# Decayed keys through DRAM in 2 KB rows and back in 512 B runs, and the state update's products in four 32-column tiles, in a new order

## The chip, the cores and the metric

One core of one Trainium2 chip. The metric is device microseconds of one execution, and lower is better. A profile's span is about 1.8 us shorter than the time of the same execution, so spans are compared with spans and times with times. The *granted clock* is TensorE's clock in a trace as a share of full speed. The *slack* of a chunk is the other work that TensorE has between the write of its keys and their use.

## The reference, cut to what matters

```python
# q, k, v, alpha: (4, 8, 768, 48); w_in: 384 x 2048; w_out: 2048 x 384
for t in range(S):
    state = alpha[:, :, t, :, None] * state + np.einsum('bhd,bhe->bhde', k[:, :, t], v[:, :, t])
    y[:, :, t] = np.einsum('bhd,bhde->bhe', q[:, :, t], state)
# x = y as (3072 tokens, 384)
h = x @ w_in
g = h * np.clip(h + 3.0, 0.0, 6.0) / 6.0
return g @ w_out
```

The kernel works in 24 chunks of 128 tokens, six to a batch. For each chunk the recurrence needs a product of the decayed keys and the values, summed over tokens: the *update*, called `u` below. The keys come out of the decay with the head dimension on the partitions, and the update needs tokens there. So the keys must be turned. The two large products over `w_in` and `w_out` fill most of TensorE's time, and the recurrence is woven between them.

## The kernel before: the parts that matter

Chunks 0 to 4 turn their keys on TensorE (`k_by_token`, `keep_k`); chunk 5, like the last chunk of every batch, needs no update. Chunks from `FAR` on turn 32x32 blocks on VectorE (`turn_k`) and let the DMA carry the blocks to their places: out to DRAM (`write_k`), and back (`read_k`).

```python
    FAR = 6
    # V = 4 blocks of BLK = 32; C = 128; NP = 4 pairs of heads
    def write_k(j):
        far_t[j] = far.tile([BLK, V, NP, V, BLK], FP, tag="far", name="far")
        src = k_in_blocks(j).rearrange("r (v p c) -> r (v p) c", v=V, p=NP)
        to = far_t[j].rearrange("s v p o c -> o s (v p) c")
        for o in range(V):
            nc.sync.dma_start(out=to[o], in_=src[BLK * o : BLK * (o + 1)])

    def read_k(j):
        kb_t[j] = wk.tile([C, NP, C], FP, tag="kb", name="kb")
        nc.sync.dma_start(out=kb_t[j].rearrange("s p r -> s (p r)"),
                          in_=far_t.pop(j).rearrange("s v p o c -> v s (p o c)"))

    def update(j):
        ...
        for p in range(NP):
            for a in range(2):
                nc.tensor.matmul(u[64 * a : 64 * a + D, p, D * a : D * a + D],
                                 kb_t[j][:, p, 64 * a : 64 * a + D],
                                 vs[:, 2 * p + a, (64 - D) * a : (64 - D) * a + D],
                                 start=True, stop=True)
```

So 256 KB go out in four DMAs of 128 B runs, and come back in one DMA of 2 KB rows. The order of everything, on all engines and queues, is one hand-made list of short names (`lk.2` loads chunk 2's keys, `u.8` is chunk 8's update, `z` is a run of dummy matmuls that keep TensorE busy).

Of the kernel before, what the change touches and what calls it, by code (L numbers as in the profile page):

```python
# [8 lines left out]
FP = mybir.dt.float32  # L9
# [8 lines left out]
def kernel(  # L18
# [32 lines left out]
    nc = tc.nc  # L51
    B, H, S, D = q.shape
    NTOK, DM = out.shape
    C = 128
    NC = S // C
    NCH = B * NC
    NP = H // 2
# [3 lines left out]
    G = 2  # L61
# [310 lines left out]
    FAR = 6  # L372
# [9 lines left out]
    def write_k(j):  # L382
        far_t[j] = far.tile([BLK, V, NP, V, BLK], FP, tag="far", name="far")
        src = k_in_blocks(j).rearrange("r (v p c) -> r (v p) c", v=V, p=NP)
        to = far_t[j].rearrange("s v p o c -> o s (v p) c")
        for o in range(V):
            nc.sync.dma_start(out=to[o], in_=src[BLK * o : BLK * (o + 1)])

    def read_k(j):
        kb_t[j] = wk.tile([C, NP, C], FP, tag="kb", name="kb")  # L390
        nc.sync.dma_start(out=kb_t[j].rearrange("s p r -> s (p r)"),
                          in_=far_t.pop(j).rearrange("s v p o c -> v s (p o c)"))
# [8 lines left out]
    def update(j):  # L401
        if last(j):
            return
        u = bank("u", j).rearrange("r p n -> r (p n)")[:, 0 : NP * 2 * D].rearrange(
            "r (p n) -> r p n", p=NP)
        ps_t["u", j] = u
        vs = v_t[j]
        for p in range(NP):
            for a in range(2):
                nc.tensor.matmul(u[64 * a : 64 * a + D, p, D * a : D * a + D],  # L410
                                 kb_t[j][:, p, 64 * a : 64 * a + D],
                                 vs[:, 2 * p + a, (64 - D) * a : (64 - D) * a + D],
                                 start=True, stop=True)
# [323 lines left out]
    with tc.manual_schedule():  # L737
        run("""la.0 z.3.5 lq.0 lk.0 lk.1 ta.0 la.1 ca.0 tq.0 r.0 lv.0.0 tk.0 lq.2 p.0 tk.1 z.0.2
            la.2 k.0 ta.1 q.0 z.0.1 lq.1 ca.1 sc.0 r.1 la.3 tq.2 z.0.5 m.0 lv.3.1 k.1 w.1 ta.2
            p.1 tq.1 ca.2 kb.0 r.2 ck.0 ta.3 u.0 ca.3 z.0.2 q.1 sm.0 sc.1 lv.1.2 p.2 la.4 kb.1  # L740
            m.1 st.1 z.0.4 ck.1 lk.2 d2.1 r.3 yi.0 w.3 d1.1 z.0.4 d3.1 cy.0 dx.1 ta.4 yi.1 q.2
            p.3 tk.2 yx.1 lk.3 k.2 d4.1 cy.1 u.1 lv.2.0 sc.2 sm.1 w.0 st.2 fa.1.0 d2.3 m.2 d1.3
            kb.2 d3.3 fb.1 ck.2 u.2 lq.3 fr.0.1 yi.2 d4.3 sm.2 w.4 fg.0.1 tk.3 st.3 f.0.3.1 k.3
            d2.0 d1.0 d3.0 ca.4 tq.3 dx.0 lq.4 r.4 yx.2 z.0.5 la.5 q.3 cy.2 d4.0 fr.0.3 sc.3
            lk.5 fg.0.3 d2.4 kb.3 m.3 w.2 d1.4 fa.0.2 dx.4 d3.4 yi.3 p.4 tk.5 yx.3 d4.4 w.5 fb.0
            cy.3 tq.4 fr.0.0 f.1.4.3 q.4 d2.2 fg.0.0 d1.2 d3.2 lq.5 dx.2 f.1.3.0 w.6 fr.1.4 d4.2
            d2.5 fg.1.4 ta.5 fa.4.1 fr.1.3 d3.5 ca.5 d1.5 w.7 f.1.2.2 r.5 fa.2.3 d2.6 fg.1.3
            d4.5 k.5 d1.6 fb.4 d3.6 w.8 f.0.5.0 fr.0.4 fr.1.2 fg.0.4 d4.6 d2.7 fg.1.2 d1.7
            f.1.5.1 d3.7 fr.0.5 w.9 fb.2 p.5 fr.1.5 d2.8 fg.1.5 d4.7 tq.5 d1.8 f.0.6.2 fg.0.5
            lk.4 q.5 fr.0.2 d3.8 w.10 ck.3 f.1.7.1 fr.0.6 fg.0.2 d2.9 d4.8 fg.0.6 d1.9 lv.4.2  # L750
            d3.9 f.0.7.0 fr.1.7 w.11 fg.1.7 d4.9 tk.4 d2.10 u.3 k.4 fr.0.7 sc.5 d3.10 d1.10
            f.1.0.3 w.12 fg.0.7 d4.10 sm.3 b.0.0.2 m.5 d2.11 st.4 fr.1.0 lv.5.0 d3.11 d1.11 w.13
            sc.4 fg.1.0 b.1.0.1 d4.11 d2.12 m.4 d1.12 d3.12 w.14 kb.4 yi.5 ck.4 d4.12 u.4
            f.1.1.0 sm.4 d2.13 st.5 d1.13 w.15 d3.13 yx.5 fr.1.1 yi.4 cy.5 fg.1.1 d2.14 f.1.6.3
            d4.13 d1.14 lk.6 d3.14 yx.4 fr.1.6 la.6 b.1.1 cy.4 fg.1.6 d4.14 d2.15 d1.15 lq.6
            d3.15 b.0.1 xc.2.1 la.7 tk.6 d4.15 b.1.2 ca.6 x.0 b.0.2 y.1 y.5 y.6 y.2 b.1.3 y.3
            y.7 y.4 y.8 y.9 b.0.3 bo.1 y.10 so.1 y.11 y.15 y.13 P.1.1.0 bo.0 s.1.0.0 so.0
            s.1.1.1 s.1.2.2 s.1.3.3 M.2.15.3 s.1.4 P.1.0.1 x.1 y.16 P.1.3.2 x.2 K.1.0 y.0 x.3
            P.1.2 K.1.2 y.17 y.12 M.2.16 y.19 K.1.1 y.18 P.1.4 y.20 y.21 xc.2.3 y.23 xc.2.4
            G.1.0 xc.2.5 O.1.0 G.1.1 M.2.0.0 xc.2.6 O.1.1 s.1.5 P.1.6 r.6 xc.2.0 k.6 P.1.5  # L760
            xc.2.7 G.1.3 kt.6 O.1.3 xc.2.8 kw.6 tq.6 xc.2.9 y.14 M.2.7.1 n.2.0.8 xc.2.2 y.22
            M.2.1 p.6 n.2.7.9 M.2.8 lv.6.1 n.2.1.10 o.2.4.0 M.2.2 q.6 e.2.4 y.24 sc.6 n.2.2.11
            xc.2.10 G.1.2 ca.7 kr.6 O.1.2 M.2.3 m.6 lk.7 M.2.18.2 M.2.4 r.7 n.2.18.12 M.2.17
            n.2.4.13 lq.7 h.2.4 M.2.19 o.2.0.0 p.7 u.6 e.2.0 M.2.9 lq.8 h.2.0 M.2.5 tk.7 yi.6
            o.2.1.0 n.2.5.14 k.7 lk.8 e.2.1 M.2.10 tq.7 cy.6 M.2.6.0 n.2.10.15 h.2.1 M.2.11 q.7
            lv.7.0 kt.7 sc.7 n.2.11.9 sm.6 kw.7 o.2.6.0 M.2.12 m.7 st.7 n.2.12.13 o.2.7.0 M.2.13
            o.2.3.0 la.8 yi.7 o.2.5.0 n.2.13.11 o.2.3.1 e.2.5 M.2.14 o.2.2.0 e.2.3 h.2.5 yx.7
            h.2.3 kr.7 P.2.0.2 cy.7 o.2.2.1 la.9 o.2.6.1 e.2.2 o.2.7.1 e.2.6 h.2.2 M.3.15.0
            h.2.6 e.2.7 xc.3.1 P.2.1.1 K.2.0 s.2.0.12 h.2.7 s.2.2.13 s.2.1.11 xc.3.3 u.7
            s.2.3.15 P.2.3.3 s.2.4 xc.3.4 tk.8 xc.3.5 G.2.0 P.2.2 xc.3.6 K.2.2 s.2.5 O.2.0  # L770
            xc.3.0 xc.3.8 xc.3.7 tq.8 M.3.0.1 K.2.1 xc.3.9 ca.8 P.2.4 n.3.0.14 xc.3.2 r.8
            xc.3.10 M.3.1 k.8 G.2.1 M.3.16 kt.8 O.2.1 n.3.1.10 p.8 kw.8 P.2.6 ca.9 q.8 r.9 M.3.2
            G.2.3 lk.9 O.2.3 M.3.7.2 sm.7 n.3.2.8 sc.8 p.9 n.3.7.9 lq.9 M.3.3 o.3.4.0 st.8 m.8
            e.3.4 M.3.8 M.3.4 h.3.4 kr.8 P.2.5 tk.9 n.3.4.11 lv.8.2 o.3.0.0 lv.9.1 k.9 e.3.0
            kt.9 la.10 M.3.9 tq.9 M.3.5 o.3.1.0 u.8 G.2.2 n.3.5.12 q.9 lk.10 M.3.18.3 O.2.2 sm.8
            e.3.1 M.3.10 h.3.0 n.3.18.13 h.3.1 M.3.6.1 n.3.10.15 kw.9 o.3.6.0 M.3.19 ca.10 st.9
            M.3.11 o.3.5.0 M.3.17 r.10 e.3.5 n.3.11.9 sc.9 lq.10 h.3.5 o.3.7.0 M.3.12 m.9 yi.8
            n.3.12.11 o.3.7.1 kr.9 M.3.13 o.3.3.0 e.3.7 la.11 yi.9 tk.10 n.3.13.8 o.3.2.0 M.3.14
            o.3.3.1 yx.9 o.3.2.1 e.3.3 h.3.7 yx.8 cy.9 h.3.3 P.3.0.3 e.3.2 s.3.1.15 cy.8 h.3.2
            s.3.3.13 o.3.6.1 P.3.1.0 xc.4.1 K.3.0 k.10 e.3.6 xc.4.3 kt.10 h.3.6 kw.10 xc.4.4 u.9  # L780
            s.3.0.11 M.4.15.1 xc.4.5 s.3.2.8 s.3.4 M.4.0.2 P.3.2 xc.4.6 n.4.0.9 lv.10.0 p.10
            lk.11 G.3.0 s.3.5 O.3.0 M.4.1 K.3.1 xc.4.0 xc.4.8 xc.4.7 P.3.4 lq.11 tq.10 n.4.1.12
            xc.4.9 xc.4.2 xc.4.10 q.10 ca.11 kr.10 M.4.2 tk.11 lv.11.2 M.4.7.0 n.4.2.10 r.11
            M.4.16 la.12 n.4.7.14 M.4.3 tq.11 M.4.8 o.4.4.0 lk.12 M.4.4 p.11 e.4.4 u.10 k.11
            n.4.4.8 sc.10 q.11 lq.12 o.4.0.0 M.4.5 m.10 e.4.0 M.4.9 n.4.5.13 sm.9 la.13 M.4.17
            o.4.1.0 st.10 M.4.18.2 tk.12 M.4.10 sm.10 sc.11 h.4.4 h.4.0 n.4.10.14 yi.10 ca.12
            st.11 e.4.1 n.4.18.8 M.4.11 m.11 M.4.19 h.4.1 yi.11 o.4.6.0 n.4.11.10 o.4.5.0 M.4.12
            o.4.7.0 e.4.5 r.12 P.3.3.2 n.4.12.8 o.4.3.0 h.4.5 o.4.7.1 M.4.13 K.3.2 k.12 e.4.7
            P.3.5 G.3.1 n.4.13.8 kt.12 O.3.1 o.4.2.0 kw.12 p.12 P.3.6 ca.13 G.3.2 r.13 O.3.2
            lv.12.1 M.4.6.1 lk.13 G.3.3 h.4.7 O.3.3 M.4.14 s.4.1.14 o.4.2.1 yx.11 o.4.3.1 e.4.2  # L790
            lq.13 yx.10 s.4.3.11 e.4.3 P.4.0.2 h.4.2 cy.11 h.4.3 cy.10 o.4.6.1 kr.12 xc.5.1
            e.4.6 xc.5.0 xc.5.3 tq.12 lv.13.0 P.4.1.3 K.4.0 h.4.6 la.14 xc.5.4 s.4.0.15 xc.5.5
            s.4.2.8 M.5.15.1 s.4.4 lk.14 M.5.0.0 xc.5.6 P.4.2 G.4.0 n.5.0.10 s.4.5 O.4.0 xc.5.7
            xc.5.8 xc.5.2 xc.5.9 xc.5.10 q.12 M.5.1 K.4.1 tk.13 P.4.4 n.5.1.12 p.13 tq.13 M.5.2
            k.13 q.13 M.5.7.3 n.5.2.13 kt.13 M.5.16 ca.14 kw.13 n.5.7.9 M.5.3 o.5.4.0 M.5.8
            e.5.4 M.5.4 h.5.4 u.12 lq.14 n.5.4.8 sc.12 sm.12 o.5.0.0 M.5.5 st.13 m.12 e.5.0
            M.5.9 kr.13 n.5.5.11 h.5.0 M.5.17 la.15 o.5.1.0 M.5.18.0 r.14 e.5.1 M.5.10 n.5.18.9
            h.5.1 sc.13 n.5.10.8 o.5.6.0 tk.14 M.5.11 m.13 M.5.19 n.5.11.13 yi.12 o.5.7.0
# [103 lines left out]
```

## Time and profile before

| | before |
|---|---|
| median of the first four executions | 569.25 us (567.37 to 571.34) |
| profiled execution | 566.39 us, an execution apart and faster than those four; span 564.6 |
| waits of TensorE for keys read back | 2.06 us in two chunks |
| granted clock from 25 to 50 us | 0.86 |

Three executions were known when the prediction was made; their median was 570.25 us. The page and the stretches are shown in the prediction. One more line of the page counts the packets:

```profile
DMA packets 121272, 53.73 MB, mean 95 GB/s; under 512 B 80638, under 2 KB 114174, under 8 KB 121214
```

One view that the prediction did not show is of the SyncE queue around chunk 6, whose keys came too late. Its columns are start in us, length in us, queue, line, operation, output and input, and count:

```profile
132.99 3.54 SPq L387 DMA_DIRECT2D far<-kq  x4
136.62 0.57 SPq L276 DMA_DIRECT2D t<-in_v_dram  x1
137.29 0.48 SPq L277 DMA_DIRECT2D t<-in_v_dram  x1
138.23 0.65 SPq L391 DMA_DIRECT2D kb<-far  x1
```

The lengths are those of issuing alone. The read back can be issued only when the writes have landed, and the queue issues nothing else while it waits for that, here from 137.77 to 138.23 us.

### The profile page before, as it was taken

To read this page: it belongs to the slowest core of one execution; us is meant where nothing else is said; L and a number is where in the kernel's file an instruction comes from. 1 tells how busy PE (TensorE), PEld (TensorE's weight loads), DVE (VectorE), ACT (ScalarE), POOL (GpSimd) and SP (SyncE) were. 2 spreads that over 40 slices of the span, in tenths; PEclk is the share of its full clock that TensorE was granted. 3 is DMA by queue.
4 is the path that set the end of the run, shared out by engine and by line. 5 is a ranking of instruction groups with operands and counts; after the bars stand their busy time and mean duration, and the time that the engine had idled before them with its cause. 6 is when DMAs were issued, how large, how long until landed. Compare 5 with 4: busy or idle time off the path is not lost.

```text
span 564.6 us, 12762 instructions
## 1 busy us (share of the span) xinstructions
PE 553.4 (98%) x5236; PEld 513.2 (91%) x5236; DVE 470.0 (83%) x798; ACT 196.4 (35%) x348; POOL 56.0 (10%) x70
## 2 busy tenths in 40 slices
PE   8899999999899999999999999999999999999997
PEld 7688987599799989999999999999999999999997
DVE  7866997999899999998998978976999967754580
ACT  1457664112332332322422422432521422432420
POOL 2333435200001000100000000000000000000000
PEclk9979999999999999999999999999999999999999
DMA  9999677103533636264264353153154340000000
GB/s 147 188 186 168 186 230 196 52 16 63 139 90 87 145 71 155 54 139 90 60 148 107 77 121 85 20 146 78 45 129 94 83 122 8 1 22 8 1 30 21
DMA packets 121272, 53.73 MB, mean 95 GB/s; under 512 B 80638, under 2 KB 114174, under 8 KB 121214
## 3 DMA queue, kind: packets, MB, share of 16 engines
q1 hardware_dynamic: 114588, 48.19, 40.8%
q10 hardware_dynamic: 6624, 4.72, 2.5%
q8 instruction: 41, 0.67, 0.5%
q14 instruction: 19, 0.14, 0.1%
HBM read 44.24 MB, written 8.65 MB: 94 GB/s over the span
## 4 chain that ended last, share of the span: by engine, by line
PE 89%; DMA 6%; DVE 2%; SPq 1%; issue 0%; ACT 0%; DVEq 0%; ACTq 0%
PE m_ps L692 35%; PE m_ps L592 29%; PE m_ps L471 6%; PE sc_ps L346 4%; PE m_ps L509 4%; PE y_ps L440 4%; DMA rings<-in_k_dram 3%; PE y_ps L450 2%; PE m_ps L482 2%; DMA t<-in_v_dram 2%; PE u_ps L410 2%; DMA kb<-far 1%; PE tk_ps L288 1%; DMA far<-kq 1%; PE m_ps L524 0%
## 5 line engine op out<-in xcount | busy, mean ns | idle before, releaser
L692 PE MATMUL m_ps<-w,g_sb 128*128 128x192 f32 x704 | 121.2, 328 | 0.0
L692 PEld LDWEIGHTS m_ps<-w,g_sb 128*128 128x128 f32 x704 | 113.8, 190 | 2.3 <-issue 1.4
L598 ACT COPY g_sb<-m_ps 128x512 f32<-128x512 f32 x110 | 64.3, 584 | 138.3 <-PE m_ps L592 123.9
L692 PE MATMUL m_ps<-rings,g_sb 128*128 128x192 f32 x528 | 91.2, 326 | 0.0
L692 PEld LDWEIGHTS m_ps<-rings,g_sb 128*128 128x128 f32 x528 | 85.7, 190 | 0.0
L592 PE MATMUL m_ps<-xc,w 128*128 128x128 f32 x640 | 83.2, 278 | 0.2 <-ACT g_sb L598 0.2
L592 PEld LDWEIGHTS m_ps<-xc,w 128*128 128x128 f32 x640 | 77.2, 192 | 3.3 <-issue 1.4
L487 ACT ACTIVATE r<-g_sb,half 128x512 f32<-128x512 f32 x80 | 55.5, 719 | 57.0 <-DVE g_sb L529 22.8
L491 DVE SCALAR_TENSOR_TENSOR g_sb<-r,g_sb 128x512 f32<-128x512 f32 x80 | 54.5, 700 | 8.1 <-PE m_ps L692 4.8
L397 POOL TENSOR_TENSOR t<-t,R 128x384 f32<-128x384 f32 x20 | 20.9, 1043 | 383.8 <-DVE t L425 206.0
L592 PE MATMUL m_ps<-xT,raw 128*128 128x128 f32 x400 | 51.8, 276 | 0.0
L592 PEld LDWEIGHTS m_ps<-xT,raw 128*128 128x128 f32 x400 | 48.7, 192 | 0.3
L529 DVE TENSOR_TENSOR g_sb<-m_ps,g_sb 128x512 f32<-128x512 f32 x30 | 20.5, 686 | 27.2 <-ACT g_sb L598 26.5
L592 PE MATMUL m_ps<-xT,w 128*128 128x128 f32 x320 | 41.9, 278 | 0.0
L639 DVE TENSOR_TENSOR g_sb<-g_sb 128x512 f32<-128x512 f32 (+1 forms) x55 | 41.7, 796 | 0.1
L592 PEld LDWEIGHTS m_ps<-xT,w 128*128 128x128 f32 x320 | 38.2, 192 | 1.2 <-issue 0.2
L352 DVE TENSOR_TENSOR A<-sc_ps,mask 128x512 f32<-128x512 f32 x48 | 30.8, 683 | 2.7 <-PE sc_ps L346 2.4
L592 PE MATMUL m_ps<-xc,raw 128*128 128x128 f32 x240 | 32.1, 277 | 0.7 <-ACT g_sb L598 0.7
L471 PE MATMUL m_ps<-xT,w 128*128 128x256 f32 x144 | 32.7, 381 | 0.0
L315 DVE TENSOR_TENSOR_SCAN R<-t,ones 128x516 f32<-128x516 f32 x24 | 29.3, 1223 | 3.1 <-ACT t L306 2.8
L529 DVE TENSOR_TENSOR g_sb<-g_sb 128x512 f32<-128x512 f32 x40 | 27.2, 683 | 5.5 <-ACT g_sb L598 5.4
L592 PEld LDWEIGHTS m_ps<-xc,raw 128*128 128x128 f32 x240 | 29.9, 192 | 1.2 <-ACT g_sb L598 0.9
(110 smaller groups left out, 711.4 us busy)
## 6 DMA issues: line engine op xcount, KB each, us to landing
raw<-in_moe_w_out_dram SPq DMA_DIRECT2D x8, 768.0 KB
t<-in_v_dram SPq DMA_DIRECT2D x48, 96.0 KB
raw<-in_moe_w_in_dram SPq DMA_DIRECT2D x24, 192.0 KB
out_dram<-oh ACTq DMA_DIRECT2D x44, 96.0 KB
far<-kq SPq DMA_DIRECT2D x60, 64.0 KB
kb<-far SPq DMA_DIRECT2D x15, 256.0 KB
kq<-in_k_dram SPq DMA_DIRECT2D x36, 96.0 KB
aq<-in_alpha_dram SPq DMA_DIRECT2D x36, 96.0 KB
```

The source lines that it names most:

```text
L315: nc.vector.tensor_tensor_scan(out=reverse(R, n - 1, n), data0=reverse(ax, n, n), data1=reverse(ones, n, n), initial=0.0, op0=ALU.mult, op ...
L346: nc.tensor.matmul(sc[h % 2][:, h // 2], K_t[j][r, h // 2], Q_t[j][r, h // 2], start=True, stop=True)
L352: nc.vector.tensor_tensor(out=A_t[j][:, NP * o : NP * (o + 1)], in0=ps_t.pop(("sc%d" % o, j)), in1=mask.unsqueeze(1).to_broadcast([C, NP, ...
L440: nc.tensor.matmul(y_of(j, (i + 1) // 2, p), vs[:, 2 * p + a, 32 * e : 32 * e + 32], A[:, NP * a + p], start=(i % 3 == 0), stop=(i > 1 and ...
L471: nc.tensor.matmul(h[:, f], w1[:, kk, o : o + C], xT_t[g][:, kk], start=(kk == 0), stop=(kk == KT - 1))
L487: nc.scalar.activation(out=to, in_=h, func=AF.Relu, bias=half, scale=1.0 / 6.0)
L491: nc.vector.scalar_tensor_tensor(out=to, in0=r, scalar=1.0, in1=h, op0=ALU.min, op1=ALU.mult)
L529: eng.tensor_tensor(out=out, in0=in0, in1=in1, op=ALU.add if s1 > 0 else ALU.subtract)
L592: nc.tensor.matmul(acc[g][i][:, f * C : (f + 1) * C], spots[w][:, f * C : (f + 1) * C], x_of(g, x), start=(first and f == 0), stop=last, s ...
L598: nc.scalar.copy(out=slots[z], in_=acc[g][i])
L639: nc.vector.tensor_tensor(out=out, in0=in0, in1=in1, op=ALU.subtract)
L692: nc.tensor.matmul(to[g], a, rhs[:, f], start=(first and f == 0), stop=(last and f == HF - 1), skip_group_check=True)
```

## The change

Its intent is fewer and longer runs through DRAM. The keys are written as they lie, in one DMA of 128 rows of 2 KB, and come back in four DMAs of 512 B runs, one for each 32 partitions. In this form a chunk's keys lie in blocks of 32, so the update takes them in four column tiles. The far path begins at chunk 8 in place of 6, and the whole order is new.

```diff
-    FAR = 6
+    FAR = 8
     def write_k(j):
-        far_t[j] = far.tile([BLK, V, NP, V, BLK], FP, tag="far", name="far")
-        src = k_in_blocks(j).rearrange("r (v p c) -> r (v p) c", v=V, p=NP)
-        to = far_t[j].rearrange("s v p o c -> o s (v p) c")
-        for o in range(V):
-            nc.sync.dma_start(out=to[o], in_=src[BLK * o : BLK * (o + 1)])
+        far_t[j] = far.tile([C, NP * C], FP, tag="far", name="far")
+        nc.sync.dma_start(out=far_t[j], in_=k_in_blocks(j))
     def read_k(j):
-        nc.sync.dma_start(out=kb_t[j].rearrange("s p r -> s (p r)"),
-                          in_=far_t.pop(j).rearrange("s v p o c -> v s (p o c)"))
+        to = kb_t[j].rearrange("s p r -> s (p r)").rearrange("s (o w) -> s o w", o=V)
+        src = far_t.pop(j).rearrange("(o s) (v w) -> v s o w", s=BLK, v=V)
+        for n in range(V):
+            nc.sync.dma_start(out=to[BLK * n : BLK * (n + 1)], in_=src[n])
     def update(j):          # for j >= FAR
+                for o in range(V):
+                    a, n = o // 2, BLK - (o % 2) * (2 * BLK - D)
+                    nc.tensor.matmul(u[BLK * o : BLK * o + n, p, D * a : D * a + D],
+                                     far_k[:, o, p, 0:n],
+                                     vs[:, 2 * p + a, (64 - D) * a : (64 - D) * a + D],
+                                     start=True, stop=True, tile_position=(0, BLK * o))
     # ... cut: the list of the order, all of it new
```

## The prediction

> **What bounds the kernel now.** I read the page's busy shares first, then the stretches, then the matmul groups with what ended the idle time before them, then TensorE's timeline around each gap.
>
> ```profile
> span 564.6 us, 12762 instructions
> PE 553.4 (98%) x5236; PEld 513.2 (91%) x5236; DVE 470.0 (83%) x798; ACT 196.4 (35%) x348; POOL 56.0 (10%) x70
> PE 89%; DMA 6%; DVE 2%; SPq 1%; issue 0%; ACT 0%; DVEq 0%; ACTq 0%
> ```
>
> TensorE is busy 98% and carries 89% of the chain that ended last. "Busy" covers pipelined ends, so I count from start to start: the first matmul starts at 1.46 us, the last ends near 561.5, the last store takes the remaining 3.1. These 560 us are TensorE work, dummies and waits. The stretches say where it has slack (columns: PE, PEld, DVE, ACT, POOL busy, granted clock, DMA share, GB/s):
>
> ```profile
> 0.00:25.00 25.00, 20.83 (x206) 17.69 (x206) 20.69 (x37) 8.71 (x12) 6.62 (x24) 1.00 1.23 170
> 25.00:50.00 25.00, 24.42 (x301) 21.03 (x302) 15.05 (x25) 13.49 (x20) 9.64 (x6) 0.86 1.12 187
> 100.00:150.00 50.00, 48.58 (x342) 42.33 (x341) 47.74 (x75) 8.96 (x19) 2.04 (x5) 1.00 0.24 57
> 150.00:200.00 50.00, 49.19 (x502) 46.39 (x500) 49.36 (x85) 16.87 (x31) 4.24 (x3) 1.00 0.50 110
> 200.00:250.00 50.00, 48.86 (x526) 45.45 (x519) 49.06 (x85) 16.66 (x35) 2.11 (x2) 1.00 0.44 101
> 250.00:564.60 314.60, 311.54 (x2980) 299.40 (x2978) 245.79 (x434) 99.14 (x190) 9.17 (x10) 1.00 0.30 69
> ```
>
> Three regimes. To 50 us the DMA is full (share above 1) and TensorE waits or runs slow. From 100 to 250 us VectorE is as full as TensorE (49.4 of 50 us), yet TensorE still loses only a few us. From 250 us TensorE alone sets the end, and the DMA is less than half busy. The change is about the decayed keys' way through DRAM; its two visible waits are these:
>
> ```profile
> 142.89 1.06 PE L592 MATMUL m_ps<-xT,w 128*128 128x128 f32 x8
> 145.09 0.56 PE L410 MATMUL u_ps<-t,kb 128*48 128x48 f32 x16 [1.14 <-DMA kb<-far]
> 145.58 1.16 PE L592 MATMUL m_ps<-xc,w 128*128 128x128 f32 x8
> ...
> 223.02 0.56 PE L410 MATMUL u_ps<-t,kb 128*48 128x48 f32 x16 [0.92 <-DMA kb<-far]
> ```
>
> So the way through DRAM costs 1.14 + 0.92 = 2.06 us in all: chunk 6's read and chunk 10's. The same lines give what the update itself occupies: 145.09 to 145.58, 0.495 us for a chunk, and this repeats to a few ns in every chunk. The bigger single loss is early:
>
> ```profile
> 22.59 1.08 PE L440 MATMUL y_ps<-A,t 128*32 128x128 f32 x32
> 25.53 0.63 PE L288 MATMUL tk_ps<-ident,rings 128*128 128x128 f32 x4 [1.86 <-DMA rings<-in_k_dram]
> ```
>
> TensorE waits 1.86 us for chunk 2's keys, and the clock then falls: 0.86 over 25 us is 3.5 us lost.
>
> **What the Trainium skill says.** "TensorEngine Tiling (Array Packing)", section Key Properties: changing the tiling mode drains TensorE, and tiles run independently. The trace agrees with both. A run of eight 128x128 matmuls takes 0.89 us to the next of its kind, 0.99 us before the column-tiled update (about 0.093 us more), and an update, tiled too, pays a similar drain on leaving. Within the update matmul starts come in pairs 7 ns apart: two tiles at once. "TensorE: Matmul & The Clock Gate", section LDWEIGHTS: loading takes time by the number of columns, not rows, so two loads of 48 columns and four of 32 hold similar work. "DMA: Bandwidth & Descriptors", Specifications: at least 512 B a transfer for line rate. The packets of 128 B in this trace took a median of 13 ns, those of 2 KB after 130 us 84 ns: 9.8 against 24 bytes a ns, so small packets do cost more per byte here, but without a wait behind it that is free. The same page's rules call splitting a transfer by partitions pointless for bandwidth, as the pieces share the engines; the four reads of the new form do just that, so I credit them nothing.
>
> **The change part by part.** (1) Chunks 6 and 7 no longer go through DRAM but turn their keys on TensorE, as chunks 0 to 4 did: four transposes each. In the trace such a group starts at 87.64 and the next thing at 88.17, of which 0.09 is the entry into column tiles, so 0.44 us: +0.88 us on TensorE. ScalarE gains two copies of 585 ns; it is 35% busy, nothing. VectorE loses two 706 ns block transposes, 1.41 us, in the stretch where it is full.
>
> (2) The update of chunks 8 on (13 chunks, since each batch's last has none) has 16 products in four tiles in place of 8 in two. Each fp32 product is two records, so there are 8 rounds of four, where there were 8 rounds of a pair. A pair's round took 45 ns for 48 streamed columns. The token-mixing products already run in rounds of four tiles (starts 7, 7, 7, then 89 ns apart, 110 ns a round at 128 columns), so four in a round are not slower as such. I take 45 ns a round, 8 x 45 + 24 on entry + 113 to leave = 0.497 us: no change. If loading weights is what limits a round (68 ns in place of 45), it is 0.18 us a chunk, 2.4 us in all.
>
> (3) DRAM traffic: 15 chunks x (2048 packets of 128 B + 128 of 2 KB) become 13 x (128 of 2 KB + 512 of 512 B): 32,640 packets become 8,320. At 13 and 84 ns, and about 28 ns for 512 B (an estimate between the 15 ns of 192 B and the 32 ns of 640 B), 560 us of engine time become 326: 235 / 16 = 15 us of the 16 engines' time. All of it lies in a period in which the DMA is half idle. What counts is latency: for chunk 6 the first write went out at 132.99, the fourth at 135.09, the read at 138.23, and the update ran at 145.09, 12 us. One write saves about 2 us of issue; four reads cost 1.7 us more. I expect 9 to 11 us.
>
> (4) The whole order is new. Counting the built program: 31 dummy matmuls in place of 28, at 0.22 us +0.67; entries from full-array work into tiled work 67 in place of 60, at 0.093 us +0.65. All else on TensorE is the same number of the same instructions. TensorE's work therefore grows by 0.88 + 0.67 + 0.65 = 2.2 us.
>
> (5) The waits. After 50 us they sum to 3.9 us: 2.06 for the two reads and about 1.8 for ScalarE's and VectorE's results. In the new order VectorE runs 1.5 to 4 us further ahead of TensorE between 125 and 250 us of TensorE's work (summing each engine's durations along the list), and chunk 6 waits for no DRAM. Against that, four chunks (8, 12, 13, 16) have only 9.0 to 9.9 us of TensorE work between the write and the update, about what chunk 6 had when it waited. I put the waits at 2 to 3 us, a gain of 1.4.
>
> (6) The start. Chunk 2's keys are the 17th load of 192 KB instead of the 18th, at about 1.2 us each, chunks 4 and 5 load later, weight slice 0 sooner; a run of seven dummies stands after the point of the 1.86 us wait. I put it at 1 us gained, uncertain by 2 or 3 either way: one missed load costs its wait and then the clock.
>
> Sum: +2.2 - 1.4 - 1.0 = -0.2 us. As the median before is 570.25, I lean slightly on the better slack of VectorE and say 569.5 us.
>
> **Rivals.** A: the DRAM path was the limit and its relief pays fully, with 2 us of waits and the early clock loss gone too, some 6 us: 563 us. For it: the two waits named, and the low clock at 25 us. Against it: 98% busy, and 13 of the 15 chunks on that path never waited. B: a new wait takes the old one's place, because four short-slack chunks wait 1 to 2 us each and the start misses a load: 575 us. For it: four reads landing separately, the slowest counting, and the slacks above. Against it: faster writes and 2 KB rows. C: the four-tile products are bound by weight loads or by issue: +2.4 us, 572 us. For it: twice as many instructions of each kind; against it, the token-mixing rounds. D: DMA relief speeds the loads, and nothing is seen of it, since TensorE does not wait for those loads after 50 us; this is my main line.
>
> **Range and chances.** Runs of the kernel before span 567.4 to 571.3, so 2 us is noise; the start contributes 3 and the waits 2. Eight in ten: 563 to 575. Over 2% faster needs under 558.8, so 11 us, about half of everything that is not TensorE's warm work (about 22 us by my count): 0.04. Over 2% slower needs 11 us of new waits: 0.05. The rest, 0.91.
>
> **What would show it.** TensorE's share stays at 97 to 98% and matmul records rise by about 222 (16 more in each of 13 updates, 8 transposes, 6 for the dummies). The update's runs of 32 records should take 0.50 us to the next start; 0.65 or more is C. Waits named for kb<-far should fall below 2 us in total; a sum above 4 is B. Packets should fall by about 24,000 and bytes by 1 MB, with no effect on the span. The clock in the stretch from 25 to 50 us decides the start: 0.95 or more is A's half, 0.8 is B's. I would be wrong if the span moved by more than 6 us with TensorE's record spacing unchanged: then the start or a load that I did not follow has moved it.

## The result, and the profile after

| | before | after |
|---|---|---|
| first measurement, median | 569.25 us (4 runs) | 563.61 us (4 runs, 562.96 to 563.79) |
| ratio, 95% interval | | 0.9898 (0.9858 to 0.9938) |
| second measurement, median | 566.98 us (12 runs) | 563.36 us (6 runs, 563.02 to 565.18) |
| ratio, 95% interval | | 0.9939 (0.9912 to 0.9967) |

A ratio here is the mean time of one kernel's runs over that of the other's of the same rounds, so it is not quite the ratio of the medians beside it. The change gains 0.6 to 1.0%, some 3.5 to 6 us. That is within 2%, as predicted, and inside the range, but by only 0.6 us: it is 6 us below the predicted 569.5. Part of the first 5.6 us is noise of the kernel before, whose median was 2 us lower in the later rounds.

The first lines of the page after, with the chain's shares:

```profile
span 561.2 us, 13170 instructions
PE 553.9 (99%) x5458; PEld 512.6 (91%) x5458; DVE 475.2 (85%) x796; ACT 198.2 (35%) x350; POOL 52.9 (9%) x70
DMA packets 96972, 52.71 MB, mean 94 GB/s; under 512 B 49936, under 2 KB 90128, under 8 KB 96912
PE 92%; SPq 3%; DMA 2%; DVE 1%; ACT 1%; issue 0%; POOL 0%; DVEq 0%
```

Matmul records rise by 5458 - 5236 = 222 and packets fall by 24,300, both as predicted. DMA's share of the chain falls from 6% to 2%. The stretches of the same execution (columns as in the prediction):

```profile
25.00:50.00 25.00, 23.75 (x308) 19.86 (x308) 19.72 (x29) 17.47 (x23) 10.70 (x8) 1.00 1.12 187
100.00:150.00 50.00, 50.00 (x373) 44.38 (x372) 48.74 (x79) 11.02 (x22) 1.70 (x9) 1.00 0.41 101
150.00:200.00 50.00, 50.00 (x555) 46.98 (x554) 49.51 (x83) 18.22 (x36) 3.02 (x3) 1.00 0.29 78
200.00:250.00 50.00, 49.95 (x546) 46.79 (x544) 49.36 (x83) 15.65 (x30) 2.12 (x2) 1.00 0.34 82
```

From 100 to 250 us TensorE lost 1.42 + 0.81 + 1.14 = 3.37 us before (50 minus each row's first number), and loses 0.05 us now. The profiled pair gained as much in all, 564.6 to 561.2, but that the two agree is chance, as a finer ledger shows: its other terms cancel.

I tally for each kernel what TensorE's runs take from start to start when they wait for nothing and the clock is full, and call the rest lost. Work rose from 535.2 to 537.1 us. Losses to about 52 us fell from 14.1 to 11.8, from there to about 258 us from 6.4 to 3.1, and after that went from 3.05 to 3.5. In sum +1.9 - 2.3 - 3.3 + 0.4 = -3.3 us. How much is called work and how much lost depends on what a run is taken to need, by 1 us or so. Two terms stand without the tally. Counting the traces gives the work that was added: 8 more transposes, 6 more dummy records, and 67 entries into tiled work in place of 60. And TensorE's own waits after 52 us sum to 3.28 us before (2.06 for keys read back, 0.95 for ScalarE, 0.28 for VectorE), with none of 0.15 us or more after.

### The profile page after: what moved, and what is told of

It reads as the page before. It is cut to its first block, busy times and chain, and to the rows that moved or that the text cites. A ratio compares the mean times of both kernels' runs of the same rounds, so it can differ in the third digit from the quotient of the medians.

```text
span 561.2 us, 13170 instructions
## 1 busy us (share of the span) xinstructions
PE 553.9 (99%) x5458; PEld 512.6 (91%) x5458; DVE 475.2 (85%) x796; ACT 198.2 (35%) x350; POOL 52.9 (9%) x70
## 4 chain that ended last, share of the span: by engine, by line
PE 92%; SPq 3%; DMA 2%; DVE 1%; ACT 1%; issue 0%; POOL 0%; DVEq 0%
PE m_ps L701 35%; PE m_ps L601 32%; PE m_ps L480 6%; PE sc_ps L346 4%; PE y_ps L449 4%; PE m_ps L518 4%; PE y_ps L459 2%; PE m_ps L491 2%; SPq L256 1%; DMA raw<-in_moe_w_in_dram 1%; PE u_ps L413 1%; SPq L267 0%; PE u_ps L419 0%; PE kb_ps L363 0%; SPq L276 0%
## 5 line engine op out<-in xcount | busy, mean ns | idle before, releaser
L496 ACT ACTIVATE r<-g_sb,half 128x512 f32<-128x512 f32 x80 | 57.1, 722 | 73.4 <-DVE g_sb L538 27.5
L326 DVE TENSOR_TENSOR_SCAN P<-t 128x516 f32<-128x516 f32 x24 | 30.7, 1279 | 0.2
```

The source lines that it names most:

```text
L326: nc.vector.tensor_tensor_scan(out=P_t[j], data0=aX[j % 2][:, 0:n], data1=ini[j % 2], initial=0.0, op0=ALU.mult, op1=ALU.add)
L496: nc.scalar.activation(out=to, in_=h, func=AF.Relu, bias=half, scale=1.0 / 6.0)
```

## The experiments

Twelve kernels ran. The spread of the kernel before is the first thing to know, so I ran it and the change again.

**The kernel before again, no edit.**

> The kernel before, unchanged, to see how far its executions differ and where. Its profiled execution spanned 564.6 us at clock 0.994, but its median is some 3 us longer, while the executions of the kernel after lie within 0.8 us of each other at clock 0.999 to 1.0. Theory S (start): the wait of 1.86 us for chunk 2's keys lets the clock fall, for a length that varies; then the slower executions have a lower mean clock, about 0.988 to 0.990 at 568 to 571 us. Theory F (far path): the waits for the reads from DRAM vary; then the clock stays at 0.994 and the time differs all the same.

Measured: 567.36 us (565.1 to 571.13), 1.0013 of before (0.9979 to 1.0046). The profiled execution was the slowest of the six, with 16.1 us lost by 52 us against 14.1 in the first trace. Two early waits for other loads than in the first trace carry these 2 us:

```profile
23.59 1.09 PE L288 MATMUL ta_ps<-ident,rings 128*128 128x128 f32 x4 [2.28 <-DMA rings<-in_alpha_dram]
46.77 0.67 PE L288 MATMUL tk_ps<-ident,rings 128*128 128x128 f32 x4 [2.43 <-DMA rings<-in_k_dram]
```

The first trace waited 1.86 us for chunk 2's keys near 25 us, and this one for alpha and, late, for other keys. Which early load is missed changes from one execution to the next, so the start of two single traces must not be compared. The rest of the 4.7 us between the two spans is on the far path: chunk 10's update waits 2.25 us for its keys at 226.3, and right after it a run of eight matmuls takes 1.64 us in place of 0.89, as the granted clock is at half from 228.1 to 231.5 us. So a late read can cost its wait and then the clock as well, and neither theory has the scatter to itself.

**The change again, no edit.**

> The kernel after, unchanged, beside its parts in the same rounds. The new path in the old order stood at 0.993 of the kernel before. If the new order adds something of its own, the whole stands clearly below, at 0.990 or less; if the path is all of it, the two agree at 0.993.

Measured: as in the table above, and 13.6 us lost by 52 us where the first trace had 11.8. The gain is real, some 3.5 us in these rounds, and its ratio of 0.9939 is that of the path alone (0.993, next), as expected if the order adds nothing on net.

**Code or order?** The two halves apart: the new path in the old order (`FAR` left at 6), and the old path in the new order (`FAR` at 8).

```diff
 # new path, old order: on the kernel after
-    FAR = 8
+    FAR = 6
+    # ... and before's list of the order
 # old path, new order: on the kernel before
-    FAR = 6
+    FAR = 8
+    # ... and after's list of the order
```

> The new way through DRAM and the four-tile products, from chunk 6 on, in the old order of instructions. Theory F: most of the gain of 5.6 us is here: 2 us of reads waited for go, so 565 to 567 us. Theory S: the start is as before, so nothing or at most the 0.36 us of the cheaper products (15 x 0.024) and part of the 2.06 us of waits: 567 to 569 us, and as scattered as before.

> The old way through DRAM (runs of 128 B out, 2 KB back, 48-column products), from chunk 8 on, in the new order. Theory S and the order as a whole: nearly all of the gain stays, 563.5 to 565 us, clock 0.999 to 1.0. Theory F: the slack between write and update was cut to 9 to 10 us of TensorE work for four chunks, so the old path makes TensorE wait 1 to 2 us in each: 567 us or more.

Measured: new path in the old order 563.23 us (561.35 to 564.05), 0.993 (0.9904 to 0.9955); old path in the new order 576.39 us (574.77 to 579.81), 1.0169 (1.0136 to 1.0201). So the path alone gives the whole gain, and the order gives none on net. With the old path it costs 9 us. The same change of path is worth about 4 us in one order and 576.39 - 563.36 = 13 us in the other.

Chunk 6, which had waited, shows the path at work. The SyncE queue with the new path in the old order:

```profile
132.63 0.35 SPq L384 DMA_DIRECT2D far<-kq  x1
133.08 0.39 SPq L276 DMA_DIRECT2D t<-in_v_dram  x1
133.56 0.53 SPq L277 DMA_DIRECT2D t<-in_v_dram  x1
134.77 2.18 SPq L391 DMA_DIRECT2D kb<-far  x4
```

and TensorE of the same kernel (the third number group is the tile; no bracket at the end means no wait):

```profile
142.51 1.06 PE L601 MATMUL m_ps<-xT,w 128*128 128x128 f32 x8
143.49 0.54 PE L413 MATMUL u_ps<-t,kb 128*32 128x48 f32 x32
143.96 1.16 PE L601 MATMUL m_ps<-xc,w 128*128 128x128 f32 x8
```

The one write takes 0.35 us of the queue where the four spread over 3.54, it lands at 134.76, the read follows at once and has landed at 138.50. That is 5.9 us from the first issue, against 12.0 us before (132.99 to 144.95), where the update had to wait. Here it starts 5 us later than its keys, with no wait. It lasts 0.47 us to the next start (143.49 to 143.96).

The old path in the new order has the opposite picture. TensorE's and VectorE's waits for DMA in it (total, times, longest, in us):

```profile
PE u_ps L410 <- DMA kb<-far: 6.0, 4, 2.4
DVE q L292 <- DMA qq<-in_q_dram: 5.6, 4, 2.0
DVE t L292 <- DMA aq<-in_alpha_dram: 3.8, 3, 1.6
```

The kernel after has only one line left of all these:

```profile
DVE t L292 <- DMA aq<-in_alpha_dram: 0.4, 1, 0.4
```

And in the stretches of the old path in the new order the loss stands from 150 us on:

```profile
150.00:250.00 100.00, 96.85 (x1011) 90.56 (x1011) 97.05 (x163) 33.71 (x64) 4.81 (x5) 1.00 0.34 80
250.00:575.60 325.60, 316.42 (x2959) 302.44 (x2957) 247.56 (x431) 98.66 (x189) 10.62 (x10) 0.99 0.28 66
```

TensorE idles 3.15 us from 150 to 250 us, and 9.18 us after that; before, it idled 3.06 us after 250 us. Its timeline says on what. The four waits for keys are in chunks 8, 12, 13 and 16, the four with the shortest slack by the prediction. The other waits after 52 us are for VectorE, 2.95 us in three; the two longer ones, 1.31 and 1.24 us, come some 3 us after VectorE itself had waited for a load. One wait for keys, and one such pair:

```profile
339.80 0.56 PE L410 MATMUL u_ps<-t,kb 128*48 128x48 f32 x16 [1.73 <-DMA kb<-far]
379.00 1.10 DVE L292 STREAM_TRANSPOSE q<-qq 128x512 f32<-128x512 f32 x1 [2.04 <-DMA qq<-in_q_dram]
382.54 1.73 PE L692 MATMUL m_ps<-w,g_sb 128*128 128x192 f32 x9 [1.24 <-DVE oh L708]
```

And twice, after the waits for keys at 271.2 and 339.8 us, the granted clock falls: it is 0.83 from 270 to 280 and from 340 to 350 us, about 3.4 us lost by my estimate (0.17 of 20 us). After the wait of 2.42 us at 246.4 it did not fall, so a long wait does not always cost the clock. Keys 6.0, VectorE 2.95 and clock 3.4 make 12.4 of the 13 us. The new order has less slack for the path; the old one could absorb most of a slow one.

**The start.** The rival theory was that the gain is in the start, by chunk 2's keys loaded earlier. Edit: `lk.2` moved ahead in the order of the kernel before.

```diff
-  ... z.0.5 m.0 lv.3.1 k.1 w.1 ta.2 ...
-  m.1 st.1 z.0.4 ck.1 lk.2 d2.1 ...
+  ... z.0.5 m.0 lk.2 lv.3.1 k.1 w.1 ta.2 ...
+  m.1 st.1 z.0.4 ck.1 d2.1 ...
```

> The kernel before with one word moved: chunk 2's keys are loaded ahead of chunk 3's values and weight slice 1, the 11th load of 192 KB in place of the 18th. Theory S: the wait of 1.86 us goes and with it the low clock (0.86 from 25 to 50 us becomes 0.95 or more); 3 to 4 us faster, 565.5 us, and less scatter. Theory F: the start isn't what the change won; at most 1 us.

Measured: 567.26 us (563.85 to 570.13), 1.0006 (0.9969 to 1.0043). No gain, though the profiled execution had a full clock from 25 to 50 us and had lost 12.1 us by 52 us, 2 us less than the first trace of before. Another load was late in it:

```profile
23.89 0.63 PE L288 MATMUL ta_ps<-ident,rings 128*128 128x128 f32 x4 [1.49 <-DMA rings<-in_alpha_dram]
```

The same move on top of the new path in the old order was to be the best version:

> The new path in the old order (563.2 us) with chunk 2's keys loaded early, an attempt at a version that beats both. The start of the old order lost 12.1 us with the early keys and 13.7 to 16.1 without in single traces, but no time was gained by it on the kernel before (567.26 against 567.13). If that gain was lost behind the waits for DRAM, it shows now: 561 to 562.5 us, 0.990 or less. If not, 563.2 us and 0.993 as without.

Measured: 563.85 us (561.95 to 564.94), 0.9937 (0.9888 to 0.9986). No better than without the move. So an earlier load of chunk 2's keys is not the gain, and no version was found that beats the change beyond the noise.

The start as a whole is not settled by that, and the record holds more than the medians. With the mean granted clock at 0.999 or more stand 8 of 10 executions of the change (median 563.29 us), 12 of the 40 of the kernel before whose clock was listed (565.15), and 2 of 6 of the new path in the old order (561.35 and 562.52). At a full clock the change is thus only 1.9 us faster than before, and no faster than those two executions of the path alone. The new order seems to steady the clock, and to pay as much for it in TensorE's work. This is a reading of the record, not shown by a run of its own, and in the kernel before a clock lost after a late read of keys counts among the rest.

**The read back.** Which part of the path pays? First the read alone: old layout and old writes, with the read cut in four by partitions, as the change has it.

```diff
-        nc.sync.dma_start(out=kb_t[j].rearrange("s p r -> s (p r)"),
-                          in_=far_t.pop(j).rearrange("s v p o c -> v s (p o c)"))
+        to = kb_t[j].rearrange("s p r -> s (p r)")
+        src = far_t.pop(j).rearrange("s v p o c -> v s (p o c)")
+        for n in range(V):
+            nc.sync.dma_start(out=to[BLK * n : BLK * (n + 1)], in_=src[n])
```

In the new order, and in the old one:

> New order, old layout in DRAM with the writes in 128 B runs and the 48-column products; only the read of 2 KB rows is cut into four, one for each 32 partitions. Theory E (engines): the old read's outermost dimension has size 4, so 4 of the 16 DMA engines carry it and it takes 5 to 6.7 us; cut in four its outermost dimension is 32 and all 16 carry it, 3 to 4 us. Then most of the loss of the old path in the new order (576.4 against about 562) goes: 563 to 567 us. Theory W (writes): the 128 B runs are what is slow: stays above 571 us.

> The kernel before with only the read cut into four by partitions. Theory E: the waits of the updates of chunks 6 and 10 (2 to 3 us) shrink to under 0.5 us, and the kernel reaches the new path in the old order within 1 us: ratio 0.993 to 0.996. Theory W: ratio 0.998 to 1.0.

Measured: 571.09 us (570.03 to 572.77), 1.0074 (1.0041 to 1.0107) in the new order, 5.3 us less than with one read; 565.03 us (563.11 to 567.3), 0.9966 (0.9937 to 0.9995) in the old one, 2 us less than before.

The next kernel has four reads too, cut by columns, so that each still has the 4 outermost:

```diff
-            nc.sync.dma_start(out=to[BLK * n : BLK * (n + 1)], in_=src[n])
+            w = slice(C * n, C * (n + 1))
+            nc.sync.dma_start(out=to[:, w], in_=src[:, :, w])
```

> As the read cut into four in the new order, but cut by columns: four reads of 512 B runs whose outermost dimension is still 4. Theory E: each runs on the same 4 engines, so nothing is gained: 574 to 582 us. If instead the number of reads in flight or their size of 64 KB is what helps, it is as good as the cut by partitions: 563 to 567 us.

Measured: 576.88 us (575.7 to 577.7), 1.0178 (1.0144 to 1.0212): all of the gain is gone. So it is not the number of reads, which costs nothing to see (576.39 with one), but the shape of each. From the packet records of the traces, medians over the chunks:

| kernel | outermost of a read | packets of the read in flight at most | time they take | first write issued to last packet of writes | read issued to its last packet | both |
|---|---|---|---|---|---|---|
| before | 4 | 6 | 3.7 to 4.1 us | 3.87 us | 5.25 us | 9.12 us |
| by columns | 4 | 7 to 8 | 3.7 to 4.1 | 3.91 | 5.08 | 9.00 |
| by partitions | 32 | 13 to 15 | 2.05 to 2.2 | 3.84 | 3.16 | 7.00 |
| after | 32 | 18 | 2.05 to 2.2 | 1.70 | 3.17 | 4.87 |

The ranges run over the medians of the traces with that form of read, and "both" adds the two medians. In the new path in the old order and in the change with its write in four (below), the reads took longer, 2.7 to 2.9 us; I have no cause for that. Packets are of 2 KB in the first and third rows and of 512 B in the others, so it is not the size of the packets either.

This is what the Trainium skill says on the page "DMA: Bandwidth & Descriptors", section "Why a DMA increments its semaphore by 16 and not by 1": the number of DMA engines is the largest up to 16 that divides both sides' slowest dimension, so 4 for the old read and 16 for the new ones. That is theory E. The traces agree: the counts of packets in flight point that way, and the records of the reads' semaphores show it outright, for every read of all 14 traces. The semaphore of a read with 4 outermost rises five times, once 0.9 to 1.1 us after the issue and then four times as data land; that of a read with 32 outermost rises sixteen times. The prediction had read another row of that page.

**The write.** The opposite pair: the change with its reads cut by column blocks, so that each has the 4 outermost, and the change with its one write cut into four.

```diff
 # reads by columns, on the kernel after
-            nc.sync.dma_start(out=to[BLK * n : BLK * (n + 1)], in_=src[n])
+            nc.sync.dma_start(out=to[:, n], in_=src[:, :, n])
 # write in four, on the kernel after
-        nc.sync.dma_start(out=far_t[j], in_=k_in_blocks(j))
+        for o in range(V):
+            r = slice(BLK * o, BLK * (o + 1))
+            nc.sync.dma_start(out=far_t[j][r], in_=k_in_blocks(j)[r])
```

> The kernel after with its four reads cut by column blocks in place of partitions: the same bytes in the same 512 B runs and as many reads, but the outermost dimension is 4. The writes stay one of 2 KB rows. With old writes the two cuts differed by 6 us (571.1 against 576.9). Theory E: the reads fall to 4 engines and take 5 us or more each group; slower than the kernel after by 3 to 7 us: 566.5 to 570.5 us. If the number of engines were not the cause, the same as after.

> The kernel after with its one write cut into four of 32 rows, still 2 KB runs. With reads on all engines, old writes stand at 571.1 and the new one at 563.4. If the number of writes (2.6 us to issue four) is the cost, most of these 7.7 us comes back: 567 us or more. If the 128 B packets are, it stays at 563.5 to 565 us.

Measured, reads by columns: 564.94 us (564.09 to 565.79), 0.9957 (0.9903 to 1.0011); about 1 to 1.5 us worse than the change, less than expected. Write in four: 566.05 us (565.41 to 567.39), 0.9979 (0.9925 to 1.0034), about 2.5 us worse. These two were measured beside each other on another chip than the change was, so their differences from it, by ratio and by median, are good to 1 us at best.

Reads by columns on the kernel after give the sharpest contrast. There the path takes 1.70 + 5.40 = 7.10 us, as long as the 7.00 us of the old writes with reads by partitions. Yet their times are 564.9 and 571.1 us. So this length is not all: the old writes cost something else. TensorE's waits after 52 us say where: with the old writes 3.4 us for keys and 2.5 us for VectorE, with the new write 1.0 us for keys and nothing else. What they occupy of the SyncE queue is shown by three kernels, at the same place in the order. Old writes, reads by partitions:

```profile
172.50 2.67 SPq L387 DMA_DIRECT2D far<-kq  x4
176.82 1.73 SPq L394 DMA_DIRECT2D kb<-far  x4
```

The change with its write in four:

```profile
173.44 1.74 SPq L386 DMA_DIRECT2D far<-kq  x4
176.56 1.78 SPq L393 DMA_DIRECT2D kb<-far  x4
```

The kernel after:

```profile
172.89 0.35 SPq L384 DMA_DIRECT2D far<-kq  x1
175.09 1.74 SPq L391 DMA_DIRECT2D kb<-far  x4
```

From the first write to the issue of the read it is 4.32, 3.12 and 2.20 us, and the loads of q, k and alpha stand in the queue behind that. In the same sequence VectorE's waits for these loads sum to 8.6, 3.2 and 0.4 us. (With reads by columns on the kernel after it is 2.3 us.)

**The writes off the queue.** If that delay of loads is the cause, the old writes should cost little when another queue issues them. Edit, on the old writes with reads by partitions in the new order:

```diff
-            nc.sync.dma_start(out=to[o], in_=src[BLK * o : BLK * (o + 1)])
+            nc.scalar.dma_start(out=to[o], in_=src[BLK * o : BLK * (o + 1)])
```

> New order, old writes in 128 B runs, reads cut by partitions (571.1 us), and the four writes issued from ScalarE's queue in place of the sync queue. In that kernel's trace VectorE waited 8.6 us for loads of q and alpha, against 0.4 in the kernel after. Theory Q (queue): the loads come late because the in-order sync queue spends 2.6 us a chunk issuing the old writes and stands behind their landing; off that queue, VectorE's waits for loads fall under 4 us and the time to 564 to 568 us. Theory L (latency alone): the path from write to read is 7.0 us as before, and the time stays at 570 us or more. ScalarE waits at the writes for VectorE's turn and issues them itself, about 2 us a chunk, which may cost some of the gain.

Measured: 575.44 us (573.15 to 577.48), 1.0151 (1.0109 to 1.0192): slower, not faster. No wait of VectorE for a load is left in the trace, nor of TensorE for keys, which is the half that was expected. But the waits have moved to ScalarE, whose own instructions now stand behind the writes:

```profile
ACT g_sb L600 <- DMA far<-kq: 29.2, 7, 7.2
ACT r L489 <- DMA far<-kq: 7.8, 3, 3.2
```

TensorE now waits 4.3 us for ScalarE and 4.0 us for VectorE after 52 us. So this run shows that the writes in the SyncE queue held up the loads, and does not show what that was worth.

## Why the prediction was right or wrong

**Right: the bound and TensorE's work.** Step (4) had +2.2 us of TensorE work; the counts of transposes, dummies and entries came out as it said, and the tally gives +1.9 with the cheaper updates. Step (2) had 0.497 us for an update in four tiles. It takes 0.471 us, against 0.495 before: 13 x 0.024 = 0.3 us gained. Rival C, four tiles bound by weight loads at 572 us, is out. One count beside it was off: the four loads of a product have 32, 16, 32 and 16 columns, 96 in all as before, not four times 32. The traces' loads of 48, 32 and 16 columns take a median of 125, 110 and 97 ns, so they do go with the columns. The counts of packets and records came as worked out, and the 28 ns estimated for a 512 B packet were 27.

**Wrong: step (3), the length of the path.** The prediction expected 9 to 11 us for it and said of the four reads "I credit them nothing", even a cost of 1.7 us. The path takes 5.9 us for chunk 6 with the new path in the old order, and the medians of its two parts sum to 4.87 us after against 9.12 before. Two terms were missed. The read in pieces of 32 partitions goes over 16 DMA engines where the old one went over 4, which is 2.1 us off its landing and 5.8 us off the kernel with the old writes (576.88 to 571.09). And the one write of 2 KB rows lands 2.2 us sooner. I had taken a general rule about splitting for the whole story, without looking at the outermost dimension of the DMA being split.

**Wrong in size: step (5), the waits.** It kept 2 to 3 us of waits, a gain of 1.4; TensorE's waits after 52 us went from 3.28 us to none, and the ledger shows 3.3 us gained between 52 and 258 us. This follows from step (3): the four chunks with 9.0 to 9.9 us of slack wait when the path takes 9 us (6.0 us in all with the old path in the new order), and do not when it takes about 5. The prediction also dropped VectorE's waits for loads held up in the same queue, because of a sentence in rival D: "nothing is seen of it, since TensorE does not wait for those loads after 50 us". VectorE does wait for them. In the kernel before, these waits are 6.0 us, mostly late (328 and 459 us), and no wait of TensorE follows there. With the old path in the new order they sum to 9.4 us, and TensorE waits 2.95 us for VectorE there.

**Not settled by single traces: step (6), the start.** It gave -1.0 with 2 or 3 us of doubt. The profiled pair shows -2.3, a second pair 16.1 against 13.6, and both scatter with which load is missed. The two runs with earlier keys gained no time, and the clocks of all executions, above, suggest that the new order does gain at the start what step (4) costs.

**The rivals.** The prediction's main line, D, that the relief is not seen, fell; that the time still lies in the range is owed to the width of the range. A named 563 us and the right cause in its first half: the path was what limited, and the two waits it named are 2.06 of the 3.28 us that went. Its other half, the early clock, was not needed: the new path alone, with the old start, gave 563.23 us. By the sign that the prediction set (0.95 or more from 25 to 50 us) that half holds in the first trace after, with 1.00, and not in the second, with 0.93. B's new waits for keys did not come. They are just what the new order has without the new path (6.0 us of them in the four chunks that B named, and 576 us), so B was right on the short slacks and wrong on what would meet them.

**What stays open.** In the new order the old writes cost 571.09 - 563.4 = 7.7 us. The number of DMAs is worth about 2.5 of these. The rest goes with the 128 B runs, which take longer to issue (2.67 against 1.74 us for four) and to land (their packets take 2.6 us against 1.86). How this splits between late keys and late loads is read from the waits of single traces (3.4 us for keys and 2.5 us for VectorE), not shown by a time, since the run meant to show it made a new wait on ScalarE. The shares also do not add up: fast reads alone take off 5.3 us in the new order, the new write alone about 11.5 us, both 13. Once the path fits the slack, the second improvement finds little left to gain.

## What to carry to other kernels

Look at the outermost dimension of every DMA that something waits for: with 4 there, splitting by partitions sped it up here (576.88 us by columns, 571.09 by partitions); with 128 there, as in the new write, splitting only cost some 2.5 us. A slow round trip costs what the slack of the order leaves uncovered, and in some of these traces the clock after a long wait too, so try a new path in the old order and the old path in the new one before you say which of the two paid. When you ask who suffers from a full queue, follow the loads to the engine that has no slack, even if it is not the one that sets the end.

## What the Trainium skill lacked or had wrong

- "DMA: Bandwidth & Descriptors", Rules for kernel authors: the row that advises against two transfers to disjoint partition halves, since both already use all engines, holds only if the whole transfer does. Here cutting a read with 4 outermost by partitions brought its packets' time from 3.7 to 4.1 us down to 2.05 to 2.2, and the kernel from 576.88 (cut by columns) to 571.09 us. A later row of the same table says how to use all 16 engines; the two should point to each other.
- The same page, Specifications: it names 512 B for line rate, and neither there nor further on does the page give times for packets of these sizes issued from SyncE. The medians here are 13 ns for 128 B, 27 ns for 512 B and 84 ns for 2 KB on the far path (131 where the write is in four).
- "TensorEngine Tiling (Array Packing)", Key Properties: that a change of mode drains TensorE is right, but it gives no time; here 0.093 us on entry into column tiles. Going from two tiles to four cost nothing: a round of four took 43 ns where a round of two took 45.
- For what issuing costs in the SyncE queue by the shape of a DMA no page has a figure; the count per instruction on "DMA: Bandwidth & Descriptors" does not go by shape. Here it is 0.35 us for 128 rows of 2 KB, against 0.56 to 0.63 us for 512 runs of 128 B, with later loads behind it.
